# Attention with an MLP on one core: two heads at a time, or four, and eight or ten of 16 key blocks in 16-bit parts

## The chip, the core and the metric

The kernel runs on one core of a Trainium2 chip. Five engines run side by side, each with its own queue of instructions in program order: TensorE (PE, matrix products, with its weight loads shown as PEld), VectorE (DVE), ScalarE (ACT), GpSimd (POOL) and SyncE (SP, which here issues most of the DMAs). They wait for each other by semaphores. The metric is the device time of the whole program in microseconds, the median of several runs; one more execution was recorded by the hardware profiler, and the rows in this document are from it.

## What is computed

The reference, cut to what matters; `A_x` is 1 x 2048 x 640, there are 32 heads of 20 columns, and the MLP has 1536 inner columns:

```python
def _A_ref(x, wqkv, wo):
    H = 32; Dh = D // H
    q, k, v = ...                       # x @ wqkv, cut into heads
    scores = jnp.einsum("bhqd,bhkd->bhqk", q, k) * (Dh ** -0.5)
    p = _softmax(scores, axis=-1)
    o = jnp.einsum("bhqk,bhkd->bhqd", p, v)
    return (heads joined) @ wo

def _B_ref(x, w1, b1, w2, b2):
    y = _layernorm(x, axis=-1)
    h = _gelu(jnp.einsum("bsd,df->bsf", y, w1) + b1)
    return jnp.einsum("bsf,fd->bsd", h, w2) + b2

xn = _layernorm(x, axis=-1)
return x + _A_ref(xn, A_wqkv, A_wo) + _B_ref(xn, B_w1, B_b1, B_w2, B_b2)
```

All is fp32. The kernel gets near fp32 accuracy from 16-bit products by splitting numbers into a high and a low part.

## The kernel before

**Three stages.** The setup (to about 225 us of the span) normalizes x, projects it to queries, keys and values and splits the MLP's weights. The attention (to about 1275 us) goes through heads and queries, with the MLP's matrix products as filler between. The tail projects the attention's result with `wo`. In the attention everything is in an order written out by hand: the loop at L1200 emits instructions for all engines, and each engine follows its share of that order.

**Heads and queries.** Two heads make a pair (`g`, 16 pairs, `NPAIR`). `ORDER` (L39) walks the pairs: the first 12 (`TAIL`) each with both halves of the queries (`hf`, 1024 each), then the last four for half 0, then for half 1. A half has two chunks of 512 queries (`cc`). `load_stack` (L145) loads a pair's queries (`qs`) and keys (`ks`) for one visit, each head in 61 rows: three groups of 20 for the products of high and low parts, one row for a shift that keeps the exponential in range.

**Groups.** The 16 key blocks of 128 keys (`kb`) are taken in groups of `GRP` = 4: 256 groups in all. `scores` (L742) makes the scores of one key block for both heads, two products side by side, one head in rows 0 to 60 and the other in rows 64 to 124, into a PSUM tile `s` (three buffers of 128x1024), and ScalarE takes the exponential into an fp32 tile `p` (128 keys x 2 heads x 512 queries).

**P times V.** Half of the key blocks (`SPLIT`, L27: two of each four) go as 16-bit parts, the other half as fp32. For a split block the high part of `p` is its upper 16 bits, read as bf16 with no copy (`upper`); the low part is a VectorE subtraction, `rest` (L757), which writes `low`. The values of split blocks lie as two f16 parts in `vfull`, those of the others as fp32. `pv` (L767) multiplies one group: for a split block and a head, high part times both value parts and low part times the first, three 16-bit products; for another block one fp32 product. A product has 32 output rows (20 columns of the head, a column of ones for the row sum, padding), and the PSUM tile `o` (`psO`, one buffer) has four quarters of 32 rows that TensorE fills side by side. Each of the two heads has two quarters, into which its products are dealt. `src[:, v0 - PAD * (1 - q % 2) :]` moves the window so that a head's rows lie at another offset in each of its quarters.

**The order in a group.** Scores of two key blocks, `tick` (which moves the side tasks by one step each), `rest` of the group's first block, a piece of filler (`other`); then scores of two more, `tick`, `rest` of the others, and `pv` of the group before. `pv` thus runs one group behind its scores.

**After the last group of a chunk** ScalarE copies `o` to `ev` (L800), and after two chunks `unload` (L808) writes both partial results and both partial row sums to DRAM (`opart`, `lpart`). When all pairs of a unit (`UNITS`: three, at the end two pairs) are done, `finish` (L861) loads them back, adds the two halves, checks the sums, takes their reciprocal, sends it through DRAM to spread it over the rows (`rb`), multiplies, splits into two f16 parts and writes `oscr`. It is a generator in `patient`, which moves on in ticks that gave VectorE nothing else. The last unit's `finish` runs in the tail; there `rb` is made by small products.

**Filler.** `mlp` (L1070) yields pieces of `layer1` (products `pu`, then `gelu` on VectorE and ScalarE, L961) and `layer2` (products `py`, then `addup`). The order per chunk of 256 tokens (`MC`) is layer1, layer1, layer2, layer1, layer2, twice; the first chunk has no layer2 yet. `other` doles pieces out by a credit of 1.265 us a group. When the MLP is done, `projection` (L1121) follows with products `z`, a chunk of 256 tokens at a time, as soon as `ready` counts all units for it. `prep_late` (L708) splits `wo`, near the end of the attention.

## Time and profile before

| | us |
|---|---|
| median of three runs | 1337.48 |
| lowest, highest | 1333.11, 1337.88 |
| span of the profiled execution | 1337.9 |
| setup, to the first scores | 224.7 |
| attention, first scores to the last product of P times V | 224.7 to 1275.0 |
| tail | 1275.0 to 1337.9 |

The profiled execution's own time is its span; the runs agree with it within 0.4%.

How to read the rows. A group row has line, engine, operation, output<-input, shapes and count; then busy us and mean ns of one; then the engine's idle time before it and what ended that. In a row of windows come the stretch, its length, and busy us (and instructions) of PE, PEld, DVE, ACT and POOL, then the granted clock of TensorE, the DMA share and GB/s. A timeline row has start, duration, engine, line, operation, count. A chain row has start, duration and what the chain ran through. Matrix products overlap: their mean ns is longer than the distance from one to the next, so distances are taken from start to start.

### The profile page before, as it was taken

The numbers are of one execution on the slowest core, as the hardware profiler recorded it, in microseconds if no ns is written. First come the engines' busy times: TensorE is split into PE (matmuls) and PEld (weight loads), VectorE is DVE, ScalarE is ACT, GpSimd is POOL, SyncE is SP. The second block draws the span as 40 slices with busy tenths as digits, with TensorE's granted clock in tenths as the row PEclk, the third lists the DMA queues.
The fourth block names the chain that finished last, engine by engine and source line by source line (L and its number), as shares of the span: only waits on it lengthen the run. The fifth ranks groups of instructions, "written<-read, shape, count | busy, mean of one in ns | idle before, by whom it ended". The sixth has DMA issues, their size and how long they took to land.

```text
span 1337.9 us, 29042 instructions
## 1 busy us (share of the span) xinstructions
PE 1325.8 (99%) x11635; PEld 586.7 (44%) x11635; DVE 1055.1 (79%) x1431; ACT 1128.0 (84%) x1306; POOL 37.5 (3%) x86
## 2 busy tenths in 40 slices
PE   9999899999999999999999999999999999999998
PEld 6645456444434343434343443344443434333366
DVE  7656754998788989878897879888879888997742
ACT  7844334999999999999999999999999999999900
POOL 3010000000000000000000000000000000000000
PEclk9999899999999999999999999999999999999999
DMA  9778723021203232212322132223032323334375
GB/s 279 254 196 176 136 79 104 15 59 39 66 28 103 61 83 81 63 48 59 111 63 81 33 93 66 75 69 94 19 80 71 93 66 87 118 95 118 105 218 188
DMA packets 100326, 129.54 MB, mean 97 GB/s; under 512 B 24292, under 2 KB 66664, under 8 KB 100188
## 3 DMA queue, kind: packets, MB, share of 16 engines
q1 hardware_dynamic: 96652, 120.25, 31.6%
q0 software_dynamic: 2912, 6.90, 2.8%
q8 instruction: 92, 1.51, 0.5%
q10 hardware_dynamic: 624, 0.51, 0.1%
q14 instruction: 46, 0.38, 0.1%
HBM read 82.14 MB, written 42.51 MB: 93 GB/s over the span
## 4 chain that ended last, share of the span: by engine, by line
PE 87%; DVE 6%; DMA 4%; ACT 1%; issue 1%; SPq 0%; ACTq 0%; DVEq 0%
PE o L779 30%; PE s L748 20%; PE py L1061 13%; PE pu L1031 11%; PE z L1146 5%; PE qkp L337 5%; PE vp L410 3%; DVE low L762 2%; DMA xt<-in_A_x_dram 1%; DMA xnt<-row 1%; DMA qkscr<-qkhl 1%; DVE st L255 1%; DVE qkhl L353 1%; ACT p L750 1%; DMA wos<-in_A_wo_dram 0%
## 5 line engine op out<-in xcount | busy, mean ns | idle before, releaser
L750 ACT ACTIVATE p<-s 128x1024 f32<-128x1024 f32 x1024 | 973.9, 1050 | 33.1 <-PE s L748 27.1
L762 DVE TENSOR_TENSOR low<-p 128x1024 f16<-128x1024 f32 x512 | 614.3, 1218 | 144.8 <-ACT p L750 144.0
L779 PE MATMUL o<-p,vfull 128*32 128x512 bf16 (+1 forms) x4096 | 429.0, 493 | 0.0
L748 PE MATMUL s<-qs,ks 61*128 61x512 f16 x2048 | 311.4, 381 | 0.2 <-ACT p L750 0.2
L748 PEld LDWEIGHTS <-ks 61*128 61x128 f16 x2048 | 61.2, 94 | 278.4 <-issue 276.1
L1061 PE MATMUL py<-w2t,hT 128*128 128x320 f16 x1152 | 178.5, 300 | 0.0
L1031 PE MATMUL pu<-xm,w1t 128*128 128x256 f16 x1440 | 178.2, 273 | 0.1
L1031 PEld LDWEIGHTS <-w1t 128*128 128x128 f16 x1440 | 131.0, 98 | 64.0 <-issue 50.2
L1061 PEld LDWEIGHTS <-hT 128*128 128x128 f16 x1152 | 102.3, 98 | 88.1 <-issue 53.9
L337 PE MATMUL qkp<-xnt,wv 128*128 128x512 f16 x600 | 131.1, 379 | 1.3 <-issue 1.3
L779 PEld LDWEIGHTS <-vfull 128*32 128x32 f16 x3072 | 59.9, 95 | 138.4 <-issue 106.9
L779 PE MATMUL o<-low,vfull 128*32 128x512 f16 x1024 | 101.3, 377 | 0.1
L337 PEld LDWEIGHTS <-wv 128*128 128x128 f16 x600 | 58.2, 98 | 71.0 <-issue 1.6
L779 PEld LDWEIGHTS o<-p,vfull 128*32 128x32 f32 x2048 | 61.7, 108 | 53.2
L410 PE MATMUL vp<-wv,xnt 128*128 128x320 f16 x480 | 69.5, 306 | 3.7 <-DVE qkhl L353 3.7
L1146 PE MATMUL z<-w1t,ot 128*128 128x320 f16 x480 | 67.4, 299 | 0.0
L352 ACT ACTIVATE qkhl<-qkp,qks 128x1024 f16<-128x1024 f32 (+1 forms) x24 | 23.1, 964 | 46.3 <-PE qkp L337 26.6
L410 PEld LDWEIGHTS <-xnt 128*128 128x128 f16 x480 | 47.9, 100 | 23.8 <-issue 3.7
L1146 PEld LDWEIGHTS <-ot 128*128 128x128 f16 x480 | 46.0, 98 | 22.9 <-issue 5.5
L353 DVE SCALAR_TENSOR_TENSOR qkhl<-qkp,qks,qkhl 128x1024 f16<-128x1024 f32 (+1 forms) x24 | 26.5, 1104 | 32.9 <-ACT qkhl L352 32.9
L1103 DVE SCALAR_TENSOR_TENSOR acc<-z,sc,acc 128x320 f32<-128x320 f32 x32 | 17.5, 549 | 37.3 <-PE z L1146 37.2
L800 ACT ACTIVATE ev<-o 128x512 f32<-128x512 f32 x64 | 39.5, 618 | 2.2 <-PE o L779 2.1
(195 smaller groups left out, 670.4 us busy)
## 6 DMA issues: line engine op xcount, KB each, us to landing
qkscr<-qkhl SPq DMA_DIRECT2D x40, 256.0 KB
opart<-ev SPq DMA_DIRECT2D x124, 80.0 KB
ks<-qkscr SPq DMA_DIRECT2D x120, 80.0 KB
qs<-qkscr SPq DMA_DIRECT2D x192, 40.0 KB
oa<-opart SPq DMA_DIRECT2D x32, 240.0 KB
xt<-in_A_x_dram SPq DMA_DIRECT2D x16, 320.0 KB
xscr<-xnt SPq DMA_DIRECT2D x4, 1280.0 KB
xm<-xscr SPq DMA_DIRECT2D x8, 640.0 KB
```

Source lines behind the costliest of these rows:

```text
L337: nc.tensor.matmul(ps[:, i, :], wv[:, k, q, a, mm * P : (mm + 1) * P], xnts[c][:, k, b, :], start=(k + n == 0), stop=(k == KD - 1 and n == 2))
L352: nc.scalar.activation(hl[:, 0, i0:i1], ps[:, i0:i1], AF.Copy, scale=a)
L353: nc.vector.scalar_tensor_tensor(hl[:, 1, i0:i1], ps[:, i0:i1], a, hl[:, 0, i0:i1], ALU.mult, ALU.subtract)
L410: nc.tensor.matmul(ps[:, hf, :320], xnts[c][:, k, a, j * P : (j + 1) * P], wv[:, k, 2, b, hf * 320 : (hf + 1) * 320], start=(n == 0), stop ...
L748: nc.tensor.matmul(ps[:, a, :], ks[64 * a : 64 * a + 61, kb * P : (kb + 1) * P], qs[64 * a : 64 * a + 61, cc * 512 : (cc + 1) * 512], star ...
L750: nc.scalar.activation(pt, ps, AF.Exp, scale=QS)
L762: nc.vector.tensor_sub(low, pt, upper(pt))
L779: nc.tensor.matmul(pv.o[32 * q : 32 * q + 32, :], src[:, v0 - PAD * (1 - q % 2) :][:, :32], t, start=q not in pv.begun, stop=last, skip_gr ...
L800: nc.scalar.activation(evs[g, hf][:, cc], pv.o, AF.Copy)
L1031: nc.tensor.matmul(ps[:, i], w1v[:, k, (f + i) // 4, a, fo_ : fo_ + P], xnt[:, k, b, :], start=(n == 0), stop=(n == 3 * KD - 1))
L1061: nc.tensor.matmul(ps[:, :320], hTs[mc][:, f, a, j * P : (j + 1) * P], w2v[:, f, b, hf * 320 : (hf + 1) * 320], start=(n == 0), stop=(n == ...
L1146: nc.tensor.matmul(ps[:, :320], ot[:, k, a, j * P : (j + 1) * P], wov[:, k, b, h * 320 : (h + 1) * 320], start=(n == 0), stop=(n == 3 * KD ...
```

## The change

Four heads at a time. `VISITS` takes the place of `ORDER`: eight quads of heads (`NQ`), the first six (`LATE`) each with all four chunks of 512 queries, then the last two for chunks 0 and 1, then for chunks 2 and 3. A group is two key blocks (`GRP` = 2) of four heads, so there are again 256 groups, each with four pairs of score products. Each head has one quarter of `o` for itself, so nothing is added up afterwards and `opart`, `lpart` and `linv` lose a dimension. `SPLIT` is now 1 0 1 0 1 1 1 0, twice: ten of 16 key blocks go as 16-bit parts. `p` and `low` are 128x4x512, with four and two buffers (before 128x2x512, with seven and four).

```diff
-SPLIT = (1, 1, 0, 0) * (NKB // 4)
+SPLIT = ((1, 0) * 2 + (1, 1) + (1, 0)) * 2
-GRP = 4
+GRP = 2
+VISITS = ([(q, tuple(range(NCC))) for q in range(LATE)]
+          + [(q, ccs) for ccs in ((0, 1), (2, 3)) for q in range(LATE, NQ)])
...
+            def rest(unit):
+                kb, pt = unit[2:]
+                if SPLIT[kb]:
+                    low = ptp.tile([P, 4, 512], F16, tag="low", name="low", bufs=2)
+                    nc.vector.tensor_sub(low, pt, upper(pt))
...
+                def products(src, at, t):
+                    for h in range(4):
+                        nc.tensor.matmul(pv.o[32 * h : 32 * h + 32, :], src[:, at(h) : at(h) + 32], t[:, h],
+                                         start=not pv.begun, stop=last, skip_group_check=True)
+                    pv.begun = True
+                split = [u for u in units if SPLIT[u[2]]]
+                for u in split:
+                    for s in range(2):
+                        products(vhalf, of16(u[2], s), upper(u[3]))
+                for u in split:
+                    products(vhalf, of16(u[2], 0), u[4])
+                for u in units:
+                    if not SPLIT[u[2]]:
+                        products(vfull, lambda h: PAD + u[2] * VROW + (4 * q + h) * VW, u[3])
...
+                    for kb in range(kb0, kb0 + GRP):
+                        pt = ptp.tile([P, 4, 512], F32, tag="p", name="p")
+                        units.append([v, cc, kb, pt])
+                        for pair in range(2):
+                            scores(v, cc, kb, pair, pt)
+                        tick()
+                        if kb % GRP == 0:
+                            if prev and SPLIT[prev[1][2]]:
+                                rest(prev[1])
+                            credit += rate
+                            other()
+                        else:
+                            if SPLIT[kb - 1]:
+                                rest(units[0])
+                            if prev:
+                                pv(prev)
```

So the second key block of a group, where it is split, gets its `low` in the next group, after that group's first scores and tick; `pv` of the group follows in the same next group.

Loads: `load_queries` brings four heads' queries for 512 queries at a time, six loads of two heads each and two single rows; `load_keys` brings the keys in two halves of eight key blocks, asked for in the first and in the fifth group of a chunk. `finish` runs per unit and chunk of 512 queries (24 times, not 12), with one load of results and no addition. `ready` counts by chunk of 256 tokens, so that `projection` waits for its own chunk's queries only. In the last `finish` the results come straight from `ev`, and `rb` takes eight small products where it took 16. `ones` moved to a pool of the setup. The branch for inputs out of range (`general`) follows the new `SPLIT`; it isn't taken.

More of the change, by code (lines that the diff above doesn't have):

```diff
@@ L168, in load_features, with load_first @@
+        def load_first():
+            parts = load_queries(0, 0), load_keys(0, 0)
+            for _ in range(8):
+                for p in parts:
+                    next(p, None)
+                yield
+            yield from load_keys(0, 1)
         def load_features(mc):
@@ L783, in pv @@
-                split = [(u[3], upper(u[4]), u[5]) for u in units if SPLIT[u[3]]]
-                whole = [(u[3], u[4]) for u in units if not SPLIT[u[3]]]
-                of16 = lambda kb, a: 2 * PAD + kb * 2 * VROW + (2 * g + a) * 2 * VW
-                of32 = lambda kb, a: PAD + kb * VROW + (2 * g + a) * VW
-                for kb, up, _ in split:
-                    for a in range(2):
-                        product(2 * a, vhalf, of16(kb, a), up[:, a])
-                        product(2 * a + 1, vhalf, of16(kb, a) + VW, up[:, a])
```

345 lines of the change are left out of this document (146 added, 199 removed).

## The prediction

> **What bounds the kernel now.** I read the page first: the busy shares, the slices, the chain that ended last.
>
> ```profile
> span 1337.9 us, 29042 instructions
> PE 1325.8 (99%) x11635; PEld 586.7 (44%) x11635; DVE 1055.1 (79%) x1431; ACT 1128.0 (84%) x1306; POOL 37.5 (3%) x86
> ...
> PE   9999899999999999999999999999999999999998
> ...
> DVE  7656754998788989878897879888879888997742
> ACT  7844334999999999999999999999999999999900
> ...
> PE 87%; DVE 6%; DMA 4%; ACT 1%; issue 1%; SPq 0%; ACTq 0%; DVEq 0%
> ```
>
> TensorE is full in every slice and carries 87% of the chain. From the seventh slice to the 38th (the attention) ScalarE is nearly full too, VectorE at eight tenths. Busy time alone does not say who sets the pace, so I asked for the chain by window, at the start of the attention and in its middle, and for the attention's busy sums.
>
> ```profile
> by line: DVE low L762 23.7%; PE pu L1031 16.0%; PE o L779 13.6%; PE s L748 11.9%; issue 5.8%; DVE hT L981 4.4%; DVE u L968 4.1%; DVE w L970 4.1%; DVE u L979 3.8%; DVE u L966 3.8%; DVE hT L980 2.9%; DVE w L972 2.4%; PE vp L410 1.6%; ACT w L9
> ...
> by line: PE o L779 39.8%; PE s L748 26.5%; PE py L1061 17.3%; PE pu L1031 16.6%
> ...
> 224.00:1275.00 1051.00, 1050.59 (x9839) 421.42 (x9838) 894.29 (x1065) 1014.98 (x1136) 15.00 (x18) 1.00 0.26 72
> ```
>
> The first row is the chain in 224 to 275 us: half of it is VectorE, the `low` subtraction (L762) with the gelu's operations. The second is 430 to 630 us: TensorE alone. The third gives busy TensorE, weight loads, VectorE, ScalarE in the attention: 1050.6, 421.4, 894.3, 1015.0 of 1051 us. So TensorE sets the pace, except while the gelus come densest (the first MLP chunk has no second layer between them); there VectorE does already. VectorE has 157 us in hand.
>
> **What the change removes on TensorE.** One group of the attention on TensorE and ScalarE:
>
> ```profile
> 706.98 0.61 PE L748 MATMUL s<-qs,ks 61*128 61x512 f16 x4
> ...
> 707.47 1.94 ACT L750 ACTIVATE p<-s 128x1024 f32<-128x1024 f32 x2 [0.20 <-PE s L748]
> ...
> 707.52 0.64 PE L779 MATMUL o<-p,vfull 128*32 128x512 bf16 x8
> 707.98 0.38 PE L779 MATMUL o<-low,vfull 128*32 128x512 f16 x4
> 708.20 1.03 PE L779 MATMUL o<-p,vfull 128*32 128x512 f32 x8
> 709.16 0.60 PE L748 MATMUL s<-qs,ks 61*128 61x512 f16 x4
> 709.70 1.81 PE L1031 MATMUL pu<-xm,w1t 128*128 128x256 f16 x15
> 711.44 0.61 PE L748 MATMUL s<-qs,ks 61*128 61x512 f16 x4
> ```
>
> Start to start, eight bf16 products take 0.46 us, four f16 products 0.22, four fp32 products (two records each) 0.96: four quarters at once, 0.23 us a set of 16-bit products. Now a group is two pairs' worth: four key blocks of two heads, 12 16-bit products and 4 fp32 ones, 1.64 us. Afterwards it is two key blocks of four heads. One split and one whole block make the same 12 and 4 (8 bf16, 4 f16, 4 fp32), so 1.64 us again. Only a group of two split blocks differs: 24 16-bit products, 0.92 + 0.44 = 1.36 us, 0.28 less. The new `SPLIT` makes one group in four such: 64 of 256, 64 x 0.285 = 18.2 us. `rb` at the end halves from 32 records, 2.43 us of the chain (the tail's rows, below): 1.2 us. The scores, the MLP's filler and the 28 of 32 projection blocks behind the attention keep their number in the program order. TensorE's gain is 19.5 us, which makes 1337.9 - 19.5 = 1318.4 us if nothing takes its place.
>
> **What it adds on VectorE.** The durations, by shape:
>
> ```profile
> L762 DVE TENSOR_TENSOR low<-p 128x1024 f16<-128x1024 f32 x512 | 614.3, 1218 | 144.8 <-ACT p L750 144.0
> L800 ACT ACTIVATE ev<-o 128x512 f32<-128x512 f32 x64 | 39.5, 618 | 2.2 <-PE o L779 2.1
> L981 DVE SCALAR_TENSOR_TENSOR hT<-u,sc,hT 128x512 f16<-128x512 f32 x48 | 36.0, 751 | 1.7
> L970 DVE TENSOR_TENSOR w<-u 128x512 f32<-128x512 f32 x48 | 33.2, 692 | 1.6
> L968 DVE TENSOR_TENSOR u<-u,b1t 128x512 f32<-128x512 f32 x48 | 33.2, 692 | 1.7
> L979 DVE SCALAR_TENSOR_TENSOR u<-w,u 128x512 f32<-128x512 f32 x48 | 33.0, 687 | 7.2 <-ACT w L977 7.1
> L972 DVE SCALAR_TENSOR_TENSOR w<-w,u 128x512 f32<-128x512 f32 x48 | 32.8, 683 | 0.0
> L966 DVE TENSOR_TENSOR u<-pu,r2f 128x512 f32<-128x512 f32 x48 | 32.8, 683 | 0.2
> ...
> L980 DVE TENSOR_SCALAR hT<-u,sc 128x512 f16<-128x512 f32 x48 | 23.4, 487 | 1.7
> ...
> L997 DVE SCALAR_TENSOR_TENSOR xb<-py,sc,xb 128x320 f32<-128x320 f32 x32 | 17.4, 544 | 0.0
> ...
> L950 DVE TENSOR_TENSOR oa<-oa 120x512 f32<-120x512 f32 x16 | 10.9, 683 | 0.0
> L952 DVE TENSOR_TENSOR oa<-oa,rb 120x512 f32<-120x512 f32 x16 | 10.9, 683 | 0.0
> L956 DVE TENSOR_TENSOR oa<-oa 120x512 f16<-120x512 f32 x16 | 10.9, 683 | 0.0
> ...
> L954 DVE CAST oa<-oa 120x512 f16<-120x512 f32 x16 | 6.7, 419 | 0.0
> ...
> L920 DVE RECIPROCAL lt<-lt 96x64 f32<-96x64 f32 x8 | 4.4, 549 | 0.3
> ```
>
> ```profile
> 255.89 0.60 DVE w L972
> 256.49 2.27 DVE low L762 x2
> 258.76 0.61 DVE u L979
> ```
>
> `low` goes from 512 of 1024 columns to 320 of 2048. That shape is not in the trace. 512 columns of the same kind (L956) take 0.683 us and 1024 take 1.218, so another 1024 add 1.07: 2.29 us alone. In the chain two follow each other in 2.27, 1.135 each, so 2.2 behind other work. I take 2.2, because the price matters only where VectorE is behind; 2.13 (two of 1.07, no fixed part) and 2.29 are the ends. 320 x 2.2 = 704 against 512 x 1.2 = 614: +90 us. The Trainium skill ("VectorE: DVE Perf Modes", section on mode 2x_2P) says that fp32 `tensor_tensor` stays at one element a cycle, 0.96 GHz; by it 2048 columns need at least 2.13 us, the sum the same within 22 us, and no faster mode rescues the larger tile. The rows' slope of 1.04 ns an element agrees.
>
> The finishing loses the sum of two halves (22 times L950's 0.68 us) and doubles its small operations on the row sums (11 to 23 times about 1 us): -15 and +12, nothing. So VectorE gets about 894 + 90 - 3 = 981 us of work at the low end, 1007 at 2.29, in 1051 - 18 = 1033 us: 95 to 97%. On the mean it fits. The question is when.
>
> **Where it doesn't fit.** I cut the changed program order into 64 blocks of four groups. A block has five `low` (kb0, kb2, kb4, kb5, kb6) and whatever gelu, `xb`, finishing and late weight work lies between them; I priced these by the rows above (a gelu is 4.68 us). A block has 1051/64 - 0.29 = 16.1 us of TensorE; the 1051 holds what is already lost there. Five `low` take 11.0, so more than 5.1 us of other work is too much. The other work is 325 us, 5.1 a block, but from 0.5 to 9.5. The first five blocks (no second layer) hold 35.6: 9.9 us too much. Of the other 59, 21 are over, by 45.1 us together, and the light ones between them can't work ahead, since `low` waits for its exponentials.
>
> How much lateness is free? One heavy block walked through, with 1.93, 2.75, 1.10, 1.93 and 0.68 us ahead of its five `low`; groups start at 0, 4.1, 8.2, 12.3. By the timeline the exponentials of a key block end 2.43 us after its scores begin (709.41 - 706.98); second blocks of a group begin at 1.9, the products at 2.46. VectorE ends the block before at 0.8; kb0's `low` at 4.9 (TensorE asks at 7.0), kb2's at 9.9 (11.1), kb4's at 13.2 (15.7), kb5's at 17.3, and TensorE asks at 15.9. It waits 1.4 of the 3.3 us excess. kb5 is the pinch: it is the second block of its group, its `low` is issued only in the next group, behind kb4's, and its product comes 1.1 us after the group's first one. Two other heavy blocks, walked so, swallow 1.7 and 1.2. I take 1.4 a block, a little under the mean, because the walk leaves out L979's waits for ScalarE's tanh (7.1 us now). Less 1.4 (or all, where less is over) the 21 blocks cost 20.1, the first five 9.9 - 1.4 = 8.5: 28.6 us. With a free 2.5 and other work 5% cheaper (rows of an engine overlap: 894 busy against 614 + 325) it is 9 us; with 2.28 and 1.0 free, 44.
>
> Sum: 1337.9 - 19.5 + 28.6 = 1347.0 us. The span of the one profiled execution lies 0.4 us above the median of the three runs, 1337.48, so I carry no correction.
>
> **The rest, at or near nothing.** `ev` leaves `psO` 32 times, not 64: 20 us of 0.618 us copies less on ScalarE, which then has 995 of 1033 us and isn't the bound; it is why I expect tanh not to be later than now. Queries now come as six loads of two heads' 512 columns, keys in halves: 192, 120 and 104 issues on SyncE as before; the first loads of a half wait until TensorE has left that half, with four groups (16 us) to land; DMA is 26% busy in the attention. Behind such a wait in SyncE's queue stand the `opart` writes and the finishing's loads, for which VectorE waits only after four ticks. `opart` traffic halves. Two more V blocks in parts cost two operations of L422's kind in the setup, under TensorE's projections. The tail stays TensorE's: `ready` by chunk lets chunks 4 and 5 go before the last `finish`, but there was no wait there to remove:
>
> ```profile
> 1275.06 9.48 PE z L1146 x69
> 1284.53 2.43 PE rb L931 x32
> 1286.97 39.63 PE z L1146 x291
> ```
>
> **Rivals.**
> 1. *TensorE stays alone: 1318 us.* For: in the middle its chain has no other engine, and VectorE averages 95 to 97% afterwards. Against: the chain in 224 to 275 us is VectorE's where both have equal work, before anything is added. It holds if the pinch at kb5 swallows 3 us rather than 1.4. The Trainium skill ("Perfetto Trace Analysis", section on identifying the most-contended engine) would choose it: it takes VectorE's occupancy over the window as a fair measure and names the engine with the highest. This trace's start speaks against an average over the window.
> 2. *VectorE is the pace wherever it is over, with nothing swallowed: 1337.9 - 19.5 + 45.1 + 9.9 = 1373 us*, and 1385 at 2.28. For: at the start it is so now. Against: light blocks lie between.
> 3. *Keys late at the nine changes of visit*, two microseconds each on top of the forecast: 1365 us. For: SyncE's queue is in order. Against: no such wait in the trace, and 16 us of room.
> 4. *The quarters don't overlap once all four have their own moving operand*: 0.23 us more on each of ten bf16 sets a block, 147 us, 1485 us. Against: the `low` and fp32 sets have four different ones already and take 0.22 a set.
>
> **Chances.** Forecast 0.55, rival 1 0.25, rival 2 0.12, rival 3 0.06, rival 4 0.02. 0.5% is 6.7 us, about what a measurement can tell from no change: under 1331, or over 1344. The forecast's own range is 1328 to 1363; of its 0.55 I put 0.03 below, 0.20 within, 0.32 above. With rival 1 faster is 0.28, same 0.20, slower 0.52. The range reaches from rival 1 to the forecast's upper end with rival 3: 1317 to 1366.
>
> **What would show it.** Right: `low` at 2.2 to 2.3 us; `o` of a two-split group at 1.36 us; VectorE above 93% in the attention and in the chain in heavy stretches; waits of the `o` products on `low`, mostly kb5's. Wrong: a chain of TensorE alone after 300 us (rival 1), or waits on `ks`. A `low` well under 2.2 us, or a free lateness above 3, would make the prediction wrong.

## The result and the profile after

The changed kernel takes 1409.49 us (median of 4 runs, 1405.95 to 1411.3), the kernel before on the same chip 1335.42: a ratio of 1.056, 95% interval 1.053 to 1.058. It is 74 us slower. The prediction had the direction, but its 1347 us and its range up to 1366 were far too low. The profiled execution spans 1409.3 us, 71.4 more than before's 1337.9.

The page of the kernel after: busy time by engine, the slices of VectorE and ScalarE, the chain that ended last, and from the groups those of the attention (busy us, mean ns of one; idle time ahead of them and what ended it).

```profile
PE 1334.5 (95%) x11875; PEld 599.2 (43%) x11875; DVE 1171.7 (83%) x1257; ACT 1126.1 (80%) x1274; POOL 39.3 (3%) x87
...
DVE  6668657998989889889898889989898889898842
ACT  6844427989998989898999899989898989898910
...
PE 65%; DVE 23%; issue 4%; ACT 3%; DMA 3%; SPq 2%; DVEq 0%; ACTq 0%
PE o L800 18%; DVE low L785 15%; PE s L772 12%; PE qkp L361 9%; PE py L1016 8%; PE pu L986 7%; PE vp L434 5%; PE z L1101 4%; ACT p L774 3%; DVE u L924 1%; DVE u L922 1%; DVE u L935 1%; DVE hT L937 1%; DMA qs<-qkscr 1%; DVE hT L936 1%
...
L774 ACT ACTIVATE p<-s 128x1024 f32<-128x1024 f32 x1024 | 976.2, 1033 | 107.0 <-PE s L772 93.3
L785 DVE TENSOR_TENSOR low<-p 128x2048 f16<-128x2048 f32 x320 | 726.6, 2282 | 55.7 <-ACT p L774 49.5
...
L800 PE MATMUL o<-low,vfull 128*32 128x512 f16 x1280 | 121.9, 381 | 64.2 <-DVE low L785 63.9
```

The first and the last of these groups on the page of the kernel before:

```profile
L750 ACT ACTIVATE p<-s 128x1024 f32<-128x1024 f32 x1024 | 973.9, 1050 | 33.1 <-PE s L748 27.1
...
L779 PE MATMUL o<-low,vfull 128*32 128x512 f16 x1024 | 101.3, 377 | 0.1
```

VectorE's slices in the attention are at nine tenths where they were at eight. The chain was 87% TensorE and 6% VectorE; now VectorE has 23%, 15% by the `low` subtraction alone. TensorE's products of `low` wait 64 us for it; before, the whole idle time ahead of them was 0.1 us. `low` takes 2.28 us. A second loss shows in the row of the exponentials: ScalarE is idle 107 us ahead of them (before 33), 93 of it for TensorE's scores (before 27). They are late because TensorE was.

The attention alone, from 219 to 1347 us after (busy TensorE, weight loads, VectorE, ScalarE; then the granted clock):

```profile
219.00:1347.00 1128.00, 1060.32 (x10089) 433.83 (x10088) 1011.68 (x891) 1012.48 (x1104) 16.33 (x17) 0.99 0.21 59
```

It grew from 1051 to 1128 us. VectorE's work is 1012 us, as the prediction's upper figure of 1007 had it, and 1012 us would have fitted in the 1033 us that the prediction gave TensorE. It didn't fit in practice: VectorE was idle for 116 us. What it was waiting for (the five longest rows of VectorE's waits in the whole run: us in total, times, the longest; the second lies mostly behind the attention, the third ahead of it):

```profile
DVE low L785 <- ACT p L774: 49.5, 42, 5.1
DVE acc L1058 <- PE z L1101: 39.3, 29, 1.9
DVE qkhl L377 <- ACT qkhl L376: 29.5, 14, 6.5
DVE xb L953 <- PE py L1016: 23.8, 19, 2.9
DVE u L922 <- PE pu L986: 20.1, 17, 2.2
```

Up to 50 us for exponentials and 44 us for TensorE's MLP products (`py`, `pu`). In the kernel before the last two were 0.0 and 0.2 us, and the wait for exponentials was 144.0: the idle column of L997, L966 and L762, shown in the prediction.

Here is one such place, VectorE's timeline first (start, us, what; in brackets the idle time ahead of it and what ended it).

```profile
804.91 2.29 DVE L785 TENSOR_TENSOR low<-p 128x2048 f16<-128x2048 f32 x1
808.71 2.29 DVE L785 TENSOR_TENSOR low<-p 128x2048 f16<-128x2048 f32 x1 [1.51 <-ACT p L774]
812.17 0.69 DVE L922 TENSOR_TENSOR u<-pu,r2f 128x512 f32<-128x512 f32 x1 [1.17 <-PE pu L986]
812.89 0.69 DVE L924 TENSOR_TENSOR u<-u,b1t 128x512 f32<-128x512 f32 x1
813.62 0.69 DVE L926 TENSOR_TENSOR w<-u 128x512 f32<-128x512 f32 x1
814.23 2.28 DVE L785 TENSOR_TENSOR low<-p 128x2048 f16<-128x2048 f32 x1
816.43 0.68 DVE L928 SCALAR_TENSOR_TENSOR w<-w,u 128x512 f32<-128x512 f32 x1
817.03 4.48 DVE L785 TENSOR_TENSOR low<-p 128x2048 f16<-128x2048 f32 x2
```

The same place in TensorE's timeline:

```profile
810.65 1.48 PE L986 MATMUL pu<-xm,w1t 128*128 128x256 f16 x12
...
815.99 0.61 PE L772 MATMUL s<-qs,ks 61*128 61x512 f16 x4
816.52 1.09 PE L800 MATMUL o<-p,vfull 128*32 128x512 bf16 x16
817.44 0.39 PE L800 MATMUL o<-low,vfull 128*32 128x512 f16 x4
819.37 0.40 PE L800 MATMUL o<-low,vfull 128*32 128x512 f16 x4 [1.54 <-DVE low L785]
```

At 819.37 TensorE starts kb5's `low` products 1.54 us late. In the 12 us before, VectorE stood still twice: 1.51 us until exponentials were there, then 1.17 us until TensorE had finished `pu`, because L922 is next in its queue. Then three steps of the gelu (to 814.3), kb4's `low`, L928, and only at 817.03 kb5's. VectorE had the time, but ahead of the rush, when its queue had nothing ready.

To sum TensorE's waits I took, over all its groups of matmuls in the attention, the distance from one start to the next less the group's usual length, and counted what exceeds 0.15 us. Before: 3.7 us in all. After: 94.6 us, of which 55.5 between kb4's and kb5's `low` products (37 of the 64 groups with two split blocks), 20.4 ahead of a group's first `low` product, 8.0 behind `py` (nearly all at a halved clock, see the end), 3.5 between `low` products and the next scores (late queries and keys: the profile puts 1.8 us of waits down to `qs` and 1.2 to `ks`), the rest in small pieces. The sums depend on the usual lengths that are taken, by some 5 us (`before_ten` below by up to 9).

These waits account for the loss. The waits grew by 94.6 - 3.7 = 90.9 us; TensorE saves 64 x 0.18 = 11.6 us of products in the attention (worked out under "Why the prediction was wrong"); that makes 79.3. From the first scores to the end of the last product of P times V the attention grew by 78.1 us, from 1050.3 to 1128.4 (219.04 to 1347.48). The span grew by less, 71.4, because the setup was 5.7 us shorter in this execution (it ends anywhere from 217 to 224 us in the runs below) and the tail 1.1.

### The profile page after: what moved, and what is told of

It reads as the page before. It is cut to its first block, busy times and chain, and to the rows that moved or that the text cites. A ratio compares the mean times of both kernels' runs of the same rounds, so it can differ in the third digit from the quotient of the medians.

```text
span 1409.3 us, 28913 instructions
## 1 busy us (share of the span) xinstructions
PE 1334.5 (95%) x11875; PEld 599.2 (43%) x11875; DVE 1171.7 (83%) x1257; ACT 1126.1 (80%) x1274; POOL 39.3 (3%) x87
## 3 DMA queue, kind: packets, MB, share of 16 engines
q8 instruction: 94, 1.54, 0.5%
## 4 chain that ended last, share of the span: by engine, by line
PE 65%; DVE 23%; issue 4%; ACT 3%; DMA 3%; SPq 2%; DVEq 0%; ACTq 0%
PE o L800 18%; DVE low L785 15%; PE s L772 12%; PE qkp L361 9%; PE py L1016 8%; PE pu L986 7%; PE vp L434 5%; PE z L1101 4%; ACT p L774 3%; DVE u L924 1%; DVE u L922 1%; DVE u L935 1%; DVE hT L937 1%; DMA qs<-qkscr 1%; DVE hT L936 1%
## 5 line engine op out<-in xcount | busy, mean ns | idle before, releaser
L774 ACT ACTIVATE p<-s 128x1024 f32<-128x1024 f32 x1024 | 976.2, 1033 | 107.0 <-PE s L772 93.3
L785 DVE TENSOR_TENSOR low<-p 128x2048 f16<-128x2048 f32 x320 | 726.6, 2282 | 55.7 <-ACT p L774 49.5
L800 PE MATMUL o<-p,vfull 128*32 128x512 bf16 (+1 forms) x4096 | 392.3, 468 | 0.0
L772 PE MATMUL s<-qs,ks 61*128 61x512 f16 x2048 | 315.2, 384 | 3.1 <-DMA qs<-qkscr 1.8
L800 PEld LDWEIGHTS <-vfull 128*32 128x32 f16 x3840 | 86.1, 95 | 246.7 <-issue 192.5
L1016 PE MATMUL py<-w2t,hT 128*128 128x320 f16 x1152 | 185.9, 308 | 0.5 <-DVE u L922 0.4
L800 PE MATMUL o<-low,vfull 128*32 128x512 f16 x1280 | 121.9, 381 | 64.2 <-DVE low L785 63.9
L800 PEld LDWEIGHTS o<-p,vfull 128*32 128x32 f32 x1536 | 47.6, 108 | 36.3
L922 DVE TENSOR_TENSOR u<-pu,r2f 128x512 f32<-128x512 f32 x48 | 32.9, 686 | 21.0 <-PE pu L986 20.1
```

What stands on the lines that cost most here:

```text
L772: nc.tensor.matmul(ps[:, a, :], ks[rows, pair, kb % 8 * P : (kb % 8 + 1) * P], qs[rows, pair, :], start=True, stop=True)
L774: nc.scalar.activation(pt[:, 2 * pair : 2 * pair + 2], ps, AF.Exp, scale=QS)
L785: nc.vector.tensor_sub(low, pt, upper(pt))
L800: nc.tensor.matmul(pv.o[32 * h : 32 * h + 32, :], src[:, at(h) : at(h) + 32], t[:, h], start=not pv.begun, stop=last, skip_group_check=True)
L922: nc.vector.tensor_mul(u, ps, r2f[:, None, :].to_broadcast([P, 2, MC]))
L1016: nc.tensor.matmul(ps[:, :320], hTs[mc][:, f, a, j * P : (j + 1) * P], w2v[:, f, b, hf * 320 : (hf + 1) * 320], start=(n == 0), stop=(n == ...
```

## The experiments

Each kernel is the changed one with the edit shown, except `before_ten`. P, C and so on are the theories named in the expectations. "Waits" are TensorE's waits in the attention, summed as above. Ratios are against the kernel before on the same chip; its medians there lie between 1332.3 and 1335.8 us, so times of different kernels compare to within some 4 us. The stretch from 219 to 1290 us is the same for all, and a slower kernel has done less of its work by its end: the column tells how full VectorE is, not how much work it has.

| kernel | us, median | ratio, 95% interval | VectorE busy of 219 to 1290 us | waits, us |
|---|---|---|---|---|
| before | 1335.42 | | 901 | 3.7 |
| after | 1409.49 | 1.053 to 1.058 | 964 | 94.6 |
| same_half | 1403.01 | 1.048 to 1.053 | 970 | 85.4 |
| deferred | 1392.71 | 1.039 to 1.045 | 976 | 77.0 |
| eight | 1343.48 | 1.004 to 1.008 | 877 | 15.9 |
| eight_double | 1403.18 | 1.047 to 1.053 | 844 | 70.7 |
| nine | 1375.09 | 1.026 to 1.034 | 926 | 54.0 |
| half_low | 1413.11 | 1.055 to 1.064 | 982 | 100.0 |
| gelu_cut | 1356.35 | 1.012 to 1.019 | 922 | 41.2 |
| pool_low | 1477.19 | 1.103 to 1.111 | 925 | 153.8 |
| before_ten | 1383.12 | 1.035 to 1.043 | 1009 | 71.8 |
| dummy | 1397.40 | 1.045 to 1.053 | 975 | 69.1 |
| nine_deferred | 1371.20 | 1.026 to 1.031 | 931 | 48.7 |
| deferred_half | 1399.72 | 1.047 to 1.054 | 993 | 86.4 |
| dummy_spread | 1387.80 | 1.036 to 1.042 | 987 | 61.0 |
| double_cut | 1372.76 | 1.025 to 1.031 | 767 | 39.8 |

### Moving kb5's subtraction, or its product

The first theory (P) was that kb5's `low` alone is the pinch: in the 60 of its groups whose `low` products could be paired off in the trace, kb5's wait was 51 us in the 36 where other VectorE work lay between kb4's and kb5's `low`, and 2 us in the 24 where none did. `same_half` takes that work away from between them; `deferred` gives kb5's product one more group of time.

```diff
 same_half: kb5's low right behind the products, no tick in between
-                            if prev and SPLIT[prev[1][2]]:
-                                rest(prev[1])
...
+                    if SPLIT[units[1][2]]:
+                        rest(units[1])
                     prev = units
```

> Ten of 16 as in the changed kernel; only the low part of a group's second split block (kb5) is issued at once behind kb4's, before the next group's tick, so that no gelu or finishing work of VectorE stands between the two. VectorE has the same work. Theory P (the pinch: TensorE waits for kb5's low part because other work is queued between kb4 and kb5; it waits 55 us there in the changed kernel, 2 us of them in the 24 blocks with nothing in between): the wait falls to 10 to 20 us and the time to 1355 to 1375. Theory C (capacity: VectorE simply has too much to do in the heavy blocks, wherever it is issued): the wait moves to other low parts, 1400 to 1412.

```diff
 deferred: kb5's low product with the next group's
+                kept = late[:]
...
+                for u in kept:
+                    products(vhalf, of16(u[2], 0), u[4])
...
-                for u in split:
+                for u in split[:1]:
                     products(vhalf, of16(u[2], 0), u[4])
+                late[:] = split[1:]
...
-                            if SPLIT[kb - 1]:
-                                rest(units[0])
...
+                    if SPLIT[kb0]:
+                        rest(units[0])
                     prev = units
```

> Ten of 16; kb5's low product goes into the next group's products of P times V, one group (about 4 us) later, and the low part of a group's first block is issued behind the products of P times V, so that the two buffers still do. VectorE's order and work are the same. Theory P: the wait at kb5 goes (55 us, and some 8 us of a halved clock behind the longest ones): 1340 to 1360. Theory C: the same lateness shows at the next low part that TensorE asks for: 1385 to 1410.

Measured: 1403.0 and 1392.7 us. P's times are missed, C's are hit. In `same_half` the waits between kb4's and kb5's products fell from 55.5 to 23.9 us, and those ahead of a group's first `low` product rose from 20.4 to 38.3. In `deferred` the first kind is gone and the second is 49.8. With ten blocks the wait moves to whichever `low` comes next: kb5 is where it shows, but taking the work away from ahead of it doesn't remove the loss.

### The two parts of the change by themselves

```diff
 eight, and eight_double
-SPLIT = ((1, 0) * 2 + (1, 1) + (1, 0)) * 2
+SPLIT = (1, 0) * (NKB // 2)
+SPLIT = (1, 1, 0, 0) * (NKB // 4)
```

> Four heads at a time, but eight of 16 key blocks as 16-bit parts, one in each group (1 0 1 0 ...): TensorE's work as before the change, VectorE's low work as before (256 of 2048 columns, 2.2 us each, 563 us, against 512 of 1.2, 614 us), no group with two split blocks. If all of the loss comes with ten (P and C alike): 1330 to 1342, before's time. Rival F (the four heads' larger tiles are late by themselves; the 20 us at first low parts stay): 1350 to 1365.

> Four heads at a time, eight of 16 as 16-bit parts, but both in the same group (1 1 0 0 ...): 128 groups with two split blocks, 128 with none; TensorE's and VectorE's work as in the run with eight apart. Theory P: twice as many pinches at 0.9 us each, less 12 us where VectorE now has time: 1335 + 100 = 1400 to 1450. Theory C: VectorE has room, 1335 to 1350.

Four heads at a time with eight split blocks cost 8 us (1343.5): just above P's and C's range, below F's figure. Its 15.9 us of waits are 7.0 at `low`, 4.3 between the fp32 products and the next scores, and small pieces. (Some expectations put `eight`'s waits at 21 us; summed as in the table they are 15.9.) So the four heads by themselves are not the loss.

`eight_double` has the same work on every engine; only the order of split and whole blocks differs. It takes 60 us more, as P said and C excluded. Busy time in 219 to 1290 us, columns as before, of `eight`:

```profile
219.00:1290.00 1071.00, 1061.92 (x9894) 427.91 (x9892) 877.12 (x830) 1007.37 (x1106) 15.12 (x17) 1.00 0.23 62
```

and of `eight_double`:

```profile
219.00:1290.00 1071.00, 1017.70 (x9407) 415.35 (x9409) 844.04 (x799) 965.94 (x1055) 13.59 (x16) 1.00 0.21 58
```

In `eight_double` VectorE is busy 844 of 1071 us, 79%, and TensorE waits 60 us between the two `low` products of a group. A group takes TensorE some 4 us; two subtractions of 2.28 us are 4.56. But that sum alone is not what costs. Two places next to each other, VectorE first:

```profile
405.32 4.49 DVE L785 TENSOR_TENSOR low<-p 128x2048 f16<-128x2048 f32 x2 [3.47 <-ACT p L774]
...
413.19 2.29 DVE L785 TENSOR_TENSOR low<-p 128x2048 f16<-128x2048 f32 x1 [0.60 <-ACT p L774]
415.54 0.69 DVE L935 SCALAR_TENSOR_TENSOR u<-w,u 128x512 f32<-128x512 f32 x1
...
416.79 0.75 DVE L937 SCALAR_TENSOR_TENSOR hT<-u,sc,hT 128x512 f16<-128x512 f32 x1
417.46 2.29 DVE L785 TENSOR_TENSOR low<-p 128x2048 f16<-128x2048 f32 x1
```

and TensorE:

```profile
409.33 1.10 PE L800 MATMUL o<-p,vfull 128*32 128x512 bf16 x16
410.25 0.61 PE L800 MATMUL o<-low,vfull 128*32 128x512 f16 x8
410.79 0.60 PE L772 MATMUL s<-qs,ks 61*128 61x512 f16 x4
...
418.37 0.39 PE L800 MATMUL o<-low,vfull 128*32 128x512 f16 x4
419.80 0.40 PE L800 MATMUL o<-low,vfull 128*32 128x512 f16 x4 [1.04 <-DVE low L785]
```

The first pair of subtractions runs back to back, ends at 409.81, and the eight products at 410.25 don't wait. In the second pair the end of a gelu stands between the two, and the second product waits 1.04 us. So it is throughout. The profile's own sum of these waits is

```profile
PE o L800 <- DVE low L785: 52.0, 46, 1.5
```

and, each second subtraction paired off with the products that need it, all of it lies in the 67 groups in which other VectorE work stands between the two subtractions; in the other 61 groups there is none. So at this load the second subtraction is late only when a piece of gelu or of the finishing stands ahead of it in the queue. Whether the same piece would make it late from another place was not tried here: `same_half`'s order, which puts nothing between, was run with ten blocks only.

The other part alone, ten split blocks in the two-head kernel before:

```diff
 before_ten, against the kernel before
-SPLIT = (1, 1, 0, 0) * (NKB // 4)
+SPLIT = (1, 1, 0, 0) * 3 + (1, 1, 1, 1)
...
-                for a in range(2):
-                    for n, (kb, _, low) in enumerate(split):
-                        product(2 * a + n % 2, vhalf, of16(kb, a), low[:, a])
+                for m in range(0, len(split), 2):
+                    for a in range(2):
+                        for n, (kb, _, low) in enumerate(split[m : m + 2]):
+                            product(2 * a + n, vhalf, of16(kb, a), low[:, a])
...
-                            rest(units[0])
+                            full = prev and all(SPLIT[u[3]] for u in prev)
+                            if not full:
+                                rest(units[0])
...
-                            for u in units[1:]:
-                                rest(u)
+                            if not full:
+                                rest(units[1])
                             if prev:
                                 pv(prev)
+                            for u in units[0 if full else 2 :]:
+                                rest(u)
```

> The kernel before, with two heads at a time as it was, and ten of 16 blocks split: every fourth group of four key blocks has four split blocks, the others two. TensorE saves 64 x 0.27 = 17.5 us (1318 us by it alone); VectorE gets 128 more subtractions of 128x1024 of 1.218 us, 156 us, 894 + 156 = 1050 us of work in an attention of about 1050 us. C (capacity with some 105 us of idling that VectorE cannot use): 1430 to 1460 us. P (64 groups with twice the subtractions due, 1 us each as with four heads): 1390 to 1415 us. T (it is the four heads' larger tiles that come too late; with two heads a subtraction can begin 1 us earlier): 1340 to 1370 us.

1383.1 us, below P and C and above T. Ten split blocks cost with two heads as well: 51 us over the kernel before on that chip (1332.3), against the 66 us from `eight` to the changed kernel with four. Its VectorE is the busiest of all, 1009 of 1071 us: with pieces of 1024 columns it is idle 62 us where the changed kernel is idle 107.

### Smaller steps: nine blocks, smaller pieces

```diff
 nine
-SPLIT = ((1, 0) * 2 + (1, 1) + (1, 0)) * 2
+SPLIT = (1, 0) * 2 + (1, 1) + (1, 0) * 5
```

> The changed kernel with nine of 16 blocks split, not ten: 32 groups with two split blocks, not 64. VectorE's work in the attention comes to 880 + 32 x 2.28 = 953 us. P (each group with two split blocks costs by itself, because two subtractions of 2.28 us fall due in one group; with ten split that was 1409 - 1343 = 66 us over 64 groups, 1.03 us each): 1343 + 33 = 1370 to 1382 us. C (capacity: TensorE waits only once VectorE's work and some 105 us of idling that it cannot use exceed TensorE's pace; 953 + 105 = 1058 us still fits in an attention of about 1055 us): the waits grow by little and TensorE saves some 9 us, 1335 to 1350 us.

1375.1 us, P's figure: half of the loss for half of the groups with two split blocks, no free first step.

```diff
 half_low
-                    nc.vector.tensor_sub(low, pt, upper(pt))
+                    for a in (0, 2):
+                        nc.vector.tensor_sub(low[:, a : a + 2], pt[:, a : a + 2], upper(pt)[:, a : a + 2])
```

> The changed kernel with each subtraction for low done as two of 128x1024, one per pair of heads, each issued at the same place; the first needs only the first pair's exponentials. By the 1.218 us of such a subtraction in the kernel before, VectorE's work grows by 640 x 1.218 - 726.6 = 53 us. S (the size of the piece matters: it can begin a micro-second earlier, and TensorE's first two products can begin after half of it): 1370 to 1395 us. C (VectorE's total sets the pace): 1409 + 53 = 1445 to 1470 us. P (groups with two split blocks, each with its extra 0.31 us): 1410 to 1440 us.

1413.1 us, in P's range (S and C are missed). The work grew only by 20 us, not 53, as the row of its `low` in the attention shows:

```profile
L786 DVE TENSOR_TENSOR low<-p 128x1024 f16<-128x1024 f32 x640 | 747.1, 1216 | 27.9 <-ACT p L774 26.3 <-PE o L801 1.0 <-issue 0.4
```

640 of 1216 ns would be 778 us; two that follow each other overlap, and the busy time is 747.1. The waits ahead of the first `low` product went from 20.4 to 1.4 us, because a first piece can start on half of the exponentials, and those between products rose from 55.5 to 71.2. Nothing is won.

`nine_deferred` and `deferred_half` combine edits already shown.

> Nine of 16 split, and the low product of the second split block of a group moved to the next group, as in deferred: 32 such places, not 64; TensorE saves 9.7 us against eight's 1343.5. P (the doubling-up is what costs, and it is gone): 1334 to 1350 us. Q (the lateness is carried on to the next subtraction as in deferred, (1392.7 - 1343.5) / 64 = 0.77 us each): 1362 to 1375 us.

> deferred (ten split, kb5's low product in the next group) with each subtraction done as two of 128x1024, each pair of heads by itself. Q (what was left in deferred is that the next subtraction begins late because it needs all four heads' exponentials; half_low's waits ahead of the first low product were 1.4 us, the changed kernel's 20.4): 1335 to 1365 us. C (VectorE's total; 747 - 727 = 20 us more work by half_low's rows): 1405 to 1430 us.

1371.2 us (Q: the lateness is carried on) and 1399.7 us (below C's range, far above Q's). Neither comes near the kernel before.

### VectorE's amount of work

```diff
 gelu_cut: three of the gelu's seven VectorE steps left out
-                nc.vector.tensor_add(u, u, b1t[:, f : f + 2, None].to_broadcast([P, 2, MC]))
-                nc.vector.tensor_mul(w, u, u)
                 yield 1.2
-                nc.vector.scalar_tensor_tensor(w, w, 1.0 / 0.044715, u, ALU.add, ALU.mult)
                 yield 0.6
...
-                nc.scalar.activation(w, w, AF.Tanh, scale=0.7978845608028654 * 0.044715)
+                nc.scalar.activation(w, u, AF.Tanh, scale=0.7978845608028654 * 0.044715)
```

> The changed kernel without three of the seven VectorE steps of the gelu (the bias, the square and the cubic factor are left out, tanh takes u itself): 48 x (0.690 + 0.692 + 0.683) = 99 us of VectorE's other work in the attention gone, the subtractions and TensorE's work as they were. C (capacity): 1011 - 99 = 912 us and some 105 us of idling fit under TensorE's pace of about 1037 us, so the waits go almost wholly: 1322 to 1340 us. P (two subtractions due in one group cost even when VectorE has time, 70.7 - 21 = 50 us over the 128 such groups of eight_double, 0.4 us each): 1345 to 1370 us.

1356.4 us. 99 us of work less take 53 us off the time, so the amount matters. But 41 us of waits stay with VectorE busy 922 of 1071 us, 25.6 of them still between kb4's and kb5's products, as P said: the amount isn't all. Here too these waits lie where other work stands between the two subtractions (by the profile's waits 21.4 us in 25 groups, 0.7 in the other 39).

Two more kernels take the two apart further. `dummy` does kb5's subtraction for nothing, in its place, with eight blocks split:

```diff
 dummy
-SPLIT = ((1, 0) * 2 + (1, 1) + (1, 0)) * 2
+SPLIT = (1, 0) * (NKB // 2)
+EXTRA = (5, 13)
...
-                if SPLIT[kb]:
+                if SPLIT[kb] or kb in EXTRA:
                     low = ptp.tile([P, 4, 512], F16, tag="low", name="low", bufs=2)
...
-                            if prev and SPLIT[prev[1][2]]:
+                            if prev and prev[1][2] in EXTRA:
```

> The changed kernel with eight of 16 split, and the subtraction for kb5 and kb13 done all the same in its place, its result used by nothing: VectorE has the work and the order of the changed kernel, TensorE that of eight (1343.5 us, waits 20.9 us), and no product is due on the second subtraction of a group. P (what costs is that the second one itself is due in the same group): the waits between low products are gone and only what the next subtraction inherits is left, 1345 to 1362 us. C (VectorE's load makes every later subtraction late, whichever product is due): 1385 to 1415 us.

1397.4 us: 54 us over `eight`, C's figure, and P is wrong that something must be due on the second subtraction. The work that nobody waits for makes the next `low` late (49.0 us of waits ahead of first `low` products).

```diff
 dummy_spread, against eight
                     unit.append(low)
+                    nc.vector.tensor_reduce(junk, pt[:, 0], AX.X, ALU.max)
```

```diff
 double_cut, against gelu_cut
-SPLIT = ((1, 0) * 2 + (1, 1) + (1, 0)) * 2
+SPLIT = (1, 1, 0, 0) * 4
```

> eight, and behind each subtraction one more VectorE instruction, a maximum over 512 columns of the same exponentials whose result is used by nothing: 256 of them at some 0.6 us (an estimate: the subtraction takes 0.57 us for 512 more columns, from 1.218 and 2.282) are 146 to 175 us, dummy's extra work of 146 us or a little more, in equal pieces in every group, and no two subtractions together. C (the amount of VectorE's work): 1385 to 1420 us, as dummy's 1397. E (two subtractions together in one group): 1343 to 1360 us.

> eight_double (eight of 16 split, two in every second group) without the three VectorE steps of the gelu left out in gelu_cut (the bias, the square and the cubic factor; tanh takes u itself): VectorE's work is about 880 - 99 = 781 us, a quarter below TensorE's pace. C (the amount): no waits to speak of, 1325 to 1345 us. E (two subtractions together): at least half of eight_double's 60 us stays, 1365 to 1400 us.

`dummy_spread`: 1387.8 us, C's range, E missed. The row of its extra instruction among VectorE's groups:

```profile
L788 DVE TENSOR_REDUCE junk<-p 128x1 f32<-128x512 f32 x256 | 173.4, 678 | 0.0
```

and its busy times from 219 to 1290 us:

```profile
219.00:1290.00 1071.00, 1029.08 (x9491) 410.81 (x9493) 987.29 (x1052) 975.32 (x1066) 13.58 (x16) 0.99 0.21 58
```

173 us of VectorE work, in equal pieces, with no two subtractions together, cost 44 us, a quarter of a microsecond for each microsecond of work. VectorE is busy 92% of the stretch.

`double_cut`: 1372.8 us, E's range, C missed. Here VectorE has a quarter of its time free, and TensorE still waits for `low`. Its busy times from 219 to 1290 us:

```profile
219.00:1290.00 1071.00, 1043.47 (x9665) 424.44 (x9663) 767.17 (x670) 990.11 (x1086) 13.62 (x16) 1.00 0.22 60
```

and the longest of TensorE's waits (us in total, times, the longest):

```profile
PE o L800 <- DVE low L785: 24.8, 28, 1.5
```

Paired off as in `eight_double`, 24.9 us of waits are in the 43 groups with other work between the two subtractions and 0.5 in the 85 without.

So each theory is right about a part. More VectorE work in total is enough to cost 44 to 54 us (`dummy_spread`, `dummy`), and two subtractions in one group, with other work queued between them, are enough to cost 60 (`eight_double`) or 38 (`double_cut`, over the kernel before); the changed kernel has both.

### The subtraction on another engine

GpSimd is 3% busy. `pool_low` is `deferred` with kb5's subtraction there:

```diff
 pool_low, against deferred
-                    nc.vector.tensor_sub(low, pt, upper(pt))
+                    (nc.gpsimd if kb % 2 else nc.vector).tensor_sub(low, pt, upper(pt))
```

> Ten of 16 split, kb5's low product moved to the next group as in deferred, and kb5's subtraction on GpSimd, not VectorE: VectorE loses 64 x 2.28 = 146 us, and two of its subtractions never fall in one group. C and P both: waits fall to about those of eight (21 us) or below, TensorE saves 18 us against eight: 1322 to 1340 us. G (no row of these traces prices such a subtraction on GpSimd; if it takes more than the 8 us of a group, or slows VectorE while it runs): 1370 us or more.

1477.2 us, the slowest of all (G). Two of its groups, GpSimd's subtraction and a step of VectorE's gelu:

```profile
L785 POOL TENSOR_TENSOR low<-p 128x2048 f16<-128x2048 f32 x64 | 278.5, 4352 | 725.9 <-ACT p L774 448.3
...
L941 DVE SCALAR_TENSOR_TENSOR u<-w,u 128x512 f32<-128x512 f32 x48 | 66.2, 1379 | 6.6 <-ACT w L939 6.5
```

One place in GpSimd's timeline:

```profile
529.20 5.15 POOL L785 TENSOR_TENSOR low<-p 128x2048 f16<-128x2048 f32 x1 [14.85 <-ACT p L774]
```

and in VectorE's at the same time:

```profile
528.61 2.28 DVE L785 TENSOR_TENSOR low<-p 128x2048 f16<-128x2048 f32 x1
530.81 4.09 DVE L941 SCALAR_TENSOR_TENSOR u<-w,u 128x512 f32<-128x512 f32 x1
534.93 0.49 DVE L942 TENSOR_SCALAR hT<-u,sc 128x512 f16<-128x512 f32 x1
```

GpSimd's subtraction takes 4.35 us (a group is 4 us of TensorE, not the 8 that the expectation names), and is hardly late itself: TensorE waits for it three times, 7.3 us in all, and 70.3 us for VectorE's:

```profile
PE o L802 <- DVE low L785: 70.3, 51, 3.3
...
PE o L802 <- POOL low L785: 7.3, 3, 3.9
```

But VectorE's L941, which reads two tiles and takes 0.68 us in the changed kernel, takes 4.09 here and ends at 534.90, half a microsecond after GpSimd's instruction (529.20 + 5.15 = 534.35). VectorE doesn't run slower beside it, it stands still until GpSimd is done. The Trainium skill ("SBUF — State Buffer", section "SBUF: two separate sides") states just that: a VectorE instruction with two SBUF inputs and a GpSimd one that reads SBUF exclude each other for a whole instruction. The trace agrees. The work left VectorE, but not its time: VectorE is busy 1189.7 us in the whole run, 1170.6 in `deferred`, though it has 64 subtractions fewer. Something else is in the loss too: `low` has two buffers, and VectorE's own subtractions wait 38.0 us for TensorE's products to free one (10.7 in `deferred`).

## Why the prediction was wrong

*What TensorE saves* (64 groups at 0.285 us, `rb` 1.2: 19.5 us) was too much. The 16 bf16 products take 0.92 us as forecast, but a two-split group that waits for nothing takes 1.46 us to the next scores (409.33 to 410.79 in `eight_double` above, and as much in the changed kernel, 324.79 to 326.25), not 1.36. Of its two sets of `low` products the first takes 0.22 us and the one just ahead of the scores 0.33; the sum took 0.22 for both, while the 0.96 us of the fp32 products, the last ones of a group before, ran to the scores' start. So a group saves 1.64 - 1.46 = 0.18 us, 64 of them 11.6, with `rb` 12.8 us: 6.7 less than forecast. That is the smaller of two errors.

*What VectorE gets* was right: 981 to 1007 us forecast, 1012 measured, `low` at 2.28 us. Against the price taken (2.2) that is 320 x 0.08 = 26 us, the upper end that was kept for the range. As a share of the longer attention it is 90%, under the 93% given as a sign.

*The mechanism* was right in kind: `o` products wait for `low`, kb5's most of all, and VectorE enters the chain. Its size was 28.6 us; the waits grew by 94.6 - 3.7 = 91. These 62 us more and the 6.7 us of TensorE's saving, less the 5.7 us of a shorter setup, are what the span of 1409.3 us lies above the forecast of 1347.0, to within some 1 us.

*The step that failed* is "Where it doesn't fit": 16.1 us a block, five `low` at 11.0, loss only where other work exceeds 5.1, and 1.4 us of lateness free in every block. That balance lets VectorE use every microsecond of a block of four groups, and lets light blocks cost nothing. By the trace:

- In the same blocks, kb5's waits are 36.9 us in the heavy ones (25 of the 60 that could be matched) and 16.4 us in the 35 light ones. The balance has 28.6 and 0.
- 20.4 us of waits ahead of a group's first `low` product are not in the sum at all, and neither are the 8.0 us behind `py`.
- VectorE was idle 116 us in an attention in which the balance, at 95 to 97%, left it some 26 to 52. Its queue is in order, and what stands next in it is often not ready: exponentials up to 50 us, TensorE's `py` and `pu` 44 us.

What the runs put in place of the balance: what counts is what stands ahead of a `low` in the queue of its group (4 us), not the sum over a block (16 us). Two subtractions that follow each other directly come in time where VectorE has room; with other work between them the second is late even with VectorE at 72% (`double_cut`). In the changed kernel, too, kb5's waits are in the groups with such work between. And at a high load lateness isn't made up before the next subtraction (`dummy`: nothing is due on the extra one, yet 54 us are lost). A late `low` holds TensorE, which holds its scores and MLP products, for which ScalarE and VectorE then wait; so VectorE's idle time isn't there to be used when it is needed. That loop is read off the waits of the three engines above; no run broke it by itself, so its share of the 71 us is not measured. Nor do VectorE's waits for `py` and `pu` by themselves show it: in `eight` they are longer, 32.4 and 45.5 us, with 15.9 us of waits on TensorE. Taking the causes away one after another gives an order of size: of the 94.6 us of waits, 53 go with 99 us of VectorE work (`gelu_cut`, 41.2 left), and 15.9 are there with eight blocks (`eight`); the 25 between are those of two subtractions in a group with other work between them. In another order the shares would differ.

*The rivals.* Rival 2 (VectorE the pace, nothing swallowed) was nearest with 1373, or 1385 at 2.28 us, and still 24 us short, since it too counts heavy blocks only. Rival 1 (TensorE alone, 1318) is refuted: its occupancy argument, by which VectorE at 95 to 97% fits, fails already at 79% in `eight_double`. The Trainium skill's rule of naming the engine with the highest occupancy ("Perfetto Trace Analysis", section "Identifying the Most-Contended Engine") gives `eight` and `eight_double` the same answer, and not VectorE: ScalarE is fuller in both, 1007 against 877 us and 966 against 844. They differ by 60 us. The rule would not have chosen rival 1 by TensorE's 99%, as the prediction has it, since it has TensorE judged by other measures than its busy time. Rival 3 (late keys) shows with at most 3.5 us of waits instead of its 18. Rival 4 (quarters that don't overlap) is refuted by the 0.92 us above.

No kernel of these beats the one before. That the tenth block could pay with a third `low` buffer, or with other VectorE work moved away from the groups with two split blocks, was not tried. `same_half`'s order with a lighter VectorE, which would show how much of the wait the order alone can remove, wasn't either.

## What to carry to other kernels

An engine that has time on the average can still set the pace: compare the work that is due with the time until it is due, and with what stands ahead of it in the queue (here two pieces of 2.28 us came in time back to back, and the second was late with a piece of gelu between them), and count the idle time of an in-order queue as lost unless the trace shows that something was ready in it. Before moving work onto a second engine, add work there that nobody needs: `dummy_spread` showed the price of 173 us, 44 us, without touching the arithmetic. And a wait that can be moved from one instruction to the next by reordering is not removed; where each move mostly shifts it, as in `same_half` and `deferred`, the load has its part in it.

## What the hardware showed that was not expected

A wait of 2.3 us can be enough to halve TensorE's clock. TensorE's timeline in the changed kernel:

```profile
448.27 0.40 PE L800 MATMUL o<-low,vfull 128*32 128x512 f16 x4 [2.30 <-DVE low L785]
...
449.19 2.85 PE L1016 MATMUL py<-w2t,hT 128*128 128x320 f16 x10
...
458.82 1.53 PE L1016 MATMUL py<-w2t,hT 128*128 128x320 f16 x10
```

and the stretch behind the wait, among its busy times (the granted clock stands third from the end):

```profile
449.20:452.20 3.00, 3.00 (x14) 1.47 (x14) 2.96 (x3) 1.83 (x2) 0.00 (x0) 0.50 0.11 33
```

Ten `py` products take 2.85 us at a clock of 0.50 and 1.53 at full clock, so the wait of 2.30 us costs 1.3 us more. Nine gaps behind `py` come to 8.0 us, nearly all of this kind.

Not every such wait does it. In this attention the clock fell seven times, at 449.02, 520.71, 592.38, 923.48, 995.16, 1066.84 and 1138.52 us; these instants lie 71.68 or 331.09 us apart, 21 or 97 times 3.413 us. Cut the attention into stretches of 3.413 us at these instants: TensorE idled 1.87 to 2.48 us in the seven stretches that ended with a fall, and at most 1.72 us in every other. Waits of 2.05 and 2.12 us (ending at 378.95 and 1279.88) that lie across such a cut did nothing. The Trainium skill ("TensorE: Matmul & The Clock Gate", section "What's actually happening") puts an idle window at about 3.4 us; the distances agree with that length, but here the clock fell after idling for little more than half of it.

And GpSimd's elementwise instruction stopped a two-input one of VectorE altogether, 4.09 us for 0.68 (`pool_low`); over the run three two-input steps of the gelu went from 0.68 and 0.69 us to means of 1.38, 1.18 and 1.01.
